# Chunk one's keys and queries by seven block products, key roundings shared between two engines, early stores in halves, and a new order of the work

## The chip, the cores and the metric

The kernel runs on one core of a Trainium2 chip. A core has five engines that run side by side, each through its own queue in order: TensorE (PE, matrix products into PSUM; its weight loads are listed apart as PEld), VectorE (DVE), ScalarE (ACT), GpSimd (POOL), and SyncE (SP), which here only issues DMAs. Semaphores order work across engines. The metric is the device time of one execution in microseconds (us), the median of several runs.

## The reference, cut to what matters

Inputs are x (2048 rows of 512), one fused weight for queries, keys and values, a small 16 x 16 weight for each of 32 heads, an output weight, the two weights of a dense layer of 1376 units, and a gate vector.

```python
qkv = (x @ wqkv) ...                                  # 32 heads of 16
pq, pk = q @ w_phi, k @ w_phi                         # per head
phi(p) = concat(softmax(p), softmax(-p))              # 32 features per head
kv, z = phi_k^T v, sum over rows of phi_k
a = (phi_q kv) / (phi_q z + 1e-6) @ wo                # linear attention
b = mish(x @ w1 + b1) @ w2                            # dense, Mish, dense
out = g * a + (1 - g) * b,  g = sigmoid(x . gate_w)
```

Everything is float32.

## The kernel before, in words

**Precision.** A float32 matrix is split into a high part (rounded to the matmul's format) and a low part (the rest). A product of two such matrices is three matmul passes: high x high, high x low, low x high. In the steps' names an h is a rounding to the high part and an l the subtraction that leaves the low part.

**Stages.** P0 prepares weights. It multiplies the key and query weights by each head's w_phi on PE (steps fk0 to fk3 and fq0 to fq3, lines 943 to 950; one for each of four row blocks of the weight, loaded by lk and lq), so that x times the fused weight gives pk or pq at once. The fused weights lie in PSUM; kh, qh round them into SBUF (line 966), kl, ql subtract (line 967), kr, qr copy them unrounded (line 970). A step's last two digits are the part (rows 0, 1, or 2 and 3 of the four) and the half r of the columns. In step, chunk 0's keys are computed as the weights come: `p0a0` is part 0, pass a (high x high; b is high x low, c is low x high), row tile 0.

Stage A goes through eight chunks of 256 rows (two tiles of 128). For each: keys k, queries q and values v (12 matmuls each per tile: three passes by four row blocks), the key features (mx, mn, d, E, S, rS, ml: maximum, minimum, differences, exp, sum, reciprocal, scaling), kv and z sums; queries are parked in DRAM (qe copies, st stores).

Stage B goes through four blocks of 512 rows: up (x @ w1, 11 units), Mish on ACT (mi), splitting (h, l), down (dn, w2), query features, numerators (nu), output product (wo), gate (gr, gs, ge, gg), the mix (ag on ACT, fi on DVE) and the stores (so, lines 890 to 892). Stage B's first units begin before stage A ends.

**Seven products.** For a chunk in FAST (line 35) keys and queries come by a scheme of seven block products (fast_ops, from line 386): with two row tiles, two halves of the 512 inner rows, and key and query weights side by side, the eight block products of the plain way become seven, s1 to s7, of 6 matmuls each. They need sums of blocks of x (sa: four additions; sh, sl: their split) and sums of blocks of the weights: t1 to t4 (lines 351 to 361), built from the unrounded copies kr and qr and split by W:h0 to h3 and W:l0 to l3. bc and m7 copy partial results on ACT; ca and qa combine them on DVE. Before, chunks 2 to 7 are in FAST; chunks 0 and 1 go the plain way.

**What sets the order.** ORDER (line 41) is a list of steps written out by hand or by a program; each engine takes its steps in the order of the list (pin, line 104). `@` gives the buffer slots that a step's new tiles take, a trailing v or g says whether VectorE or GpSimd does it, and `^` makes a GpSimd step wait until the VectorE step listed before it has ended. A tile in a reused slot waits until all readers of the slot's earlier tile are done. The loads of weights, of x and of stored results all go through SP's queue in the order of the list.

The WARM matmuls (line 192) on a tile of ones run while the first loads come.

Of the kernel before, what the change touches and what calls it, by code (L numbers as in the profile page):

```python
# [39 lines left out]
SLOTS = "01201010215"  # L40
ORDER = """
    P0| w0 lk0 lk1 fk0@01 kh00 fk1 lx0@0 xh0 kh01 kl01 kl00 p0a0@0 kr00 p0a1@1 kr01 xl0g^ lk2 fk2@23 lk3 kh10 kl10 fk3 lx1 xh1 lx2 p0b1 p0c1 kh11 kl11 p0b0 p1a1 kh20
    P0| p0c0 p1b1 xl1v p1c1 p1a0 kh21 p1b0 kl21 xh2 p1c0 p2a0 kl20 p2a1 p2b1 ldx@1 A0:xh@3467 xl2v p2c1 A0:xl0g^ kr11 A0:mn1@0 A0:d11@0 A0:mx1@0 A0:d01 kr10 lv0@0 p2b0
    P0| p2c0 A0:mx0@1 A0:d00@1 lq2 vh0 fq2@01 lq3 fq3 qr11 lq0 fq0@32 lq1 fq1 qh01 qr01 A0:xl1g A1:k0@2 A1:k1@1 qh10 qh11 ql11 A0:mn0@1 qh00 ql00 A0:ldx@0 A0:d10 lv1@1
    P0| vh1 vl0g qr10 A1:sag@1 A1:sh0 W:L1@0 vl1v A0:v1@1 A0:E0 qr00 W:t1v ql01 ql10 A0:q0@0 A0:qe0@0 W:t4v W:t3g^ A0:E1 A0:st0 A1:sh1 A1:sl0v A1:mx0@0 A1:mn0@0 A0:v0
    A1| d10@2 d00 E0 A0:ve1@3 A0:S1@0 W:h0 A0:q1@0 sl1g mx1@1 W:h1 W:t2 xh@0215 v0@3 ve0@1 A0:S0@1 A0:rS0 A0:qe1@1 A0:st1 A0:ml0v xl0v mn1@1 d11@3 xl1v W:h2 W:l2g W:l1v
    A1| q1@2 S0@1 qe1@0 A0:z0 v1@2 A2:s1@01 A2:bc@0 q0@2 ldx@1 A2:sag@0 W:H1 qe0@1 rS0 A0:ve0@2 A2:xh@3467 ml0v st0 A0:rS1 A0:ml1v A0:z1 st1 A2:xl0v A2:s6 W:h3 W:l0v
    A2| W:l3g A1:d01 s7 m7@1 ca@2 xl1g A1:E1 A1:S1@1 s2 mn0@0 v0@3 ve0@0 A3:s1@11 A1:rS1 s5 qa W:L7@1 W:H7 s4 sh0 sl0g^ A3:s7 A3:m7@0 A1:z0 A3:bc@3 s3 A1:ml1g^ A1:z1
    A2| mx0@0 sh1 W:O1g st1 mx1@1 d11@1 d10@0 A1:ve1@2 kk mn1@1 d01 E1 A3:s6 d00 E0 A3:ca@2 W:O7g^ A3:v0@1 A3:ve0@3 ldx@1 A3:xh@0251 A3:xl1g A3:sag^@0 A3:sh0 W:L2@0 W:H2
    A3| A2:v1@2 A2:ve1@1 A2:S0@0 xl0g A2:sl1v s5 s2 A2:rS0 A2:ml0v A2:z0 A2:S1@1 A2:rS1 qa st1 s4 s3 sh1 qe0@1 mn0@0 d10@2 mx1@1 d11@3 W:L0@1 sl0v mx0@0 d00 A4:s1@01  # L50
    A4| s7 bc@2 s6 A3:sl1g m7@0 A3:mn1@1 A3:d01 A3:E1 ca@1 s2 mx0@1 mn0@0 s5 qa A3:ldx@1 A2:ml1g^ A3:v1@3 A2:z1 A3:E0 st1 A3:st0 sag^@0 s4 W:H0 A3:S0@0 A3:rS0 A3:ml0g^
    A4| xh@3467 s3 sh1 A3:S1@1 A3:rS1 A3:ml1v xl0v A3:z1 sl1g xl1v A3:ve1@2 d10@0 qe0@0 d00 kk E0 v0@1 ve0@0 mn1@1 d01@1 A5:s1@22 sh0 mx1@0 v1@3 W:O0v A2:qe0@1 A2:st0
    A4| A3:z0 sl0g d11 E1 S1@0 rS1 ml1g^ z1 S0@1 A5:s7 A5:bc@1 A5:s2 A5:mn0@0 ldx@1 A5:xh@0251 A5:xl0g W:L6@1 rS0 ml0v A5:s6 A5:v1@0 A5:m7@1 A5:ca@0 W:H6 z0 A5:s5
    A5| sag^@0 s4 A4:st0 W:O2v qa s3 sh1 st1 mx0@1 d00@3 d10 xl1v A4:ve1@1 sl1g sh0 sl0v mn1@1 mx1@0 d11@2 v0@2 W:L4@0 ldx@1 qe0@0 st0 A6:s1@13 E0 S0@0 A6:sag^@0 A6:s7
    A6| bc@1 s6 m7@1 ca@2 xh@3476 A5:d01 A5:rS0 xl1g s2 A5:zld s5 qa st1 A5:E1 A5:S1@1 mn0@0 B0:LX0@1 xl0g^ A5:rS1 s4 A5:ml0v A5:ml1v sh0 sl0g s3 qe0@0 A7:s1@03 sh1
    A6| W:O6v A7:s7 A5:za A5:z0g A7:bc@1 mx0@1 st0 A7:s2 mx1@0 d11@0 A5:ve0@3 sl1v mn1@1 A5:ve1@2 kk d01 A5:z1g^ W:L8@1 A7:m7@1 A7:s6 A7:ca@2 B0:XH0 B0:XL0v v0@2 ve0@0
    A7| mx0@0 B0:LX1@0 B0:XH1 B0:XL1g^ A6:d10@1 s5 qa st1 s4 W:H4 W:H8 d00@3 W:O8g mx1@0 s3 d11@2 mn0@1 A6:v1@0 A6:d00 A6:E0 qe0@0 st0 mn1@0 d01 A6:E1 A6:S0@0 A6:rS0 E1
    A7| A6:ve1@1 W:O4g B0:lq0@1 A6:S1@1 A6:rS1 A6:ml1v B0:up1@1 B0:mi1@0 A6:ml0v W:L3@1 B0:h1@2 B0:l1v@5 A6:z0g S1@1 B0:lq2@0 B0:mx2@0 d10 v0@3 ve0@3 rS1 A6:z1v ml1g E0
    B0| A7:S0@0 A7:rS0 A7:ml0v A7:z0v up3@2 mi3@1 up0@1 mi0@0 mn2@0 A7:v1@2 A7:ve1@2 up5@0 W:L5@0 h3@3 l3v@4 ha@7 A7:z1v dn1b@1 hb@6 W:wm ph A7:zh1@10 d02v@1 A6:kv A7:kv
    B0| W:H5 dn3c@0 up2@2 dn3b mn0@1 W:H3 A7:zl1v mx0@1 pi dn0c A7:zh0 A7:zl0v A7:z0b@3 W:O5v dn1d@2 mi2@1 dn0b d00v@0 d12v A7:zc0 d10g W:O3v E0 pc A7:z1b@3 A7:zc1 T0v@1  # L60
    B0| lq1@1 mx1@0 up4@2 mn1@1 gr@0 W:L9@0 D0@0 d11g@3 dn3d dn1a@3 E2 mi4@0 dn1c h4@2 dn0ad dn3a T2v@0 up8@1 l4v@5 h2@7 l2g^@6 dn2bcd dn4d dn2a W:L10@1 W:H10 dn4c mi8@3
    B0| W:H9 h8@4 S0@1 m0 W:O9g de0 rd0 up6@2 sc0 es0v tr0 S2@0 up7@1 d01v dn4a gs up9@0 mi5@0 h5@1 l5g@7 dn5bad W:O10v E1 T1g@1 ge mi6@6 lq3@0 mn3@0 dn4b l8g^@0 dn8b
    B0| h6@3 mx3@1 d03g@2 dn5c l6g^@2 dn6ab A7:ldo@0 A7:WH1 dn6c mi7@5 h7@1 S1@1 D1@1 m1 de1 up10@2 dn6d l7g@6 dn7a W:L11@1 W:H11 B1:lq0@1 B1:mn0@1 d13g mi9@7 h9@5 st0
    B0| ld0 rd1 dn7c sc1 es1v tr1 st1 l9g^@3 dn7b dn9da D2@0 dn7d m2 de2 dn9c B1:LX0@1 rd2 W:O11v dn8c E3 dn8d A6:ldw1@1 sc2 A7:km@0 A7:kt es2v tr2 st2 dn9b mi10@2 h10@7
    B0| l10g@1 dn10a dn8a B1:lq1@0 S3@1 T3v@0 D3@1 m3 de3 rd3 sc3 es3v tr3 WL1v A7:WH0 dc A7:kc ld1 nu0@1 oh0@01 WL0v ol0 dn10bd gg0 B1:XH0 B1:XL0v dn10c ld2 wo1@0 ag1@1
    B1| B0:fi1 LX1@0 B0:wo0 d10v@0 XH1 mx1@0 d01g@3 XL1v up0@2 B0:st3 B0:ld3 B0:so1 B0:nu1@1 B0:ag0@3 B0:fi0 mn1@0 d11g B0:oh1@01 B0:ol1 E1 S1@0 up1@0 lq3@0 up2@1 mi2@6
    B1| B0:wo2 h2@2 l2g^@5 dn2ca@13 mx0@1 up6@1 d00v E0 T0g^@1 B0:ag2@2 mi1@3 dn2d@0 B0:fi2 S0@1 h1@4 l1g@0 B0:wo3@0 dn1d D0@0 dn1c mi0@7 up5@0 up3@1 hb@1 ha@6 B2:lq1@1
    B1| dn2b@2 B2:mn1@1 B2:d11v@1 ph pi pc B0:so0 dn0c T1g@0 dn0b dn1a B0:ag3@0 dn1b B0:fi3 mn3@0 B2:mx1@0 mi6@3 h6@7 B2:d01g m0 D1@1 de0 up7@0 mx3@1 l6v@2 dn6c rd0 dn6a
    B1| mi5@5 lq2@1 mn2@1 d13g@2 mx2@0 h5@3 l5g^@4 dn0a dn5b dn0d dn5d m1 de1 rd1 sc1 es1g tr1 st1 mi3@0 h3@5 dn5c l3g^@6 dn3d gr@0 dn6d B0:so2 sc0 dn3c gs dn3a up8@1
    B1| mi7@1 dn5a es0g d03v E3 S3@0 up4@2 mi8@0 h8@3 dn3b B3:lq1@0 l8v@4 dn8c d12g@3 up9@0 B2:LX0@1 tr0 d02v dn8d h7@0 l7g^@5 dn7ab T3v@0 D3@1 dn6b dn7c st0 m3 de3 rd3  # L70
    B1| up10@1 ge B3:mn1@0 sc3 E2 T2v@0 D2@0 es3g ld0 mi4@6 h4@1 l4v@7 mi10@2 h10@6 l10g@0 B2:XH0 mi9@5 S2@1 dn4d dn8a dn7d dn8b ld1 nu0@2 oh0@01 m2 dc dn4c dn10ab de2
    B1| rd2 dn10d h9@3 l9g@4 dn9adc sc2 es2v tr3 B2:LX1@0 B2:XH1 B2:XL1g dn4a B2:XL0v B2:up0@1 ol0 B2:mi0@2 wo1@0 B2:ha@5 B2:lq3@1 B2:mx3@1 dn9b B2:d03g@0 B2:mn3@1
    B2| up1@2 B1:tr2 E1 d13v E3 B1:gg0 B1:st2 B1:dn10c mi1@3 lq0@1 mx0@0 mn0@1 d10g@3 T1v@1 B1:ag1@1 B1:wo0 B1:ag0@3 up3@2 mi3@4 pc B1:st3 B1:ld2 B1:ld3 B1:nu1@0 B1:dn4b
    B2| B1:oh1@01 B1:fi1 B1:fi0 up5@2 B1:so0 B1:ol1 h1@6 l1g^@0 dn1d@2 S1@0 hb@1 B3:d11g@2 dn1c@3 h3@7 l3v@3 B1:wo3@0 mi5@4 B1:wo2 B1:ag3@2 B1:fi3 dn1b@0 T3g^@0 up4@2 pi
    B2| ph dn0cb D1@1 d00g^ m1 de1 E0 rd1 T0g@1 up2@0 sc1 es1g dn0a@1 B1:ag2@3 B1:fi2 gr@1 D3@0 gs mi4@2 B1:so2 S3@1 m3 dn0d de3 up8@1 ge dn1a rd3 sc3 h5@5 l5v@1 dn5a
    B2| up6@2 mi6@4 dn3b tr1 dn5b S0@0 dn5d h6@6 D0@1 m0 de0 rd0 sc0 dn3c es0g^ dn5c dn3da B3:LX0@0 up10@2 h4@0 l4g^@5 dn4b mi2@1 h2@7 es3v dn4c l2g^@2 dn4d lq2@1 mx2@1
    B2| mn2@1 d12g^@1 dn2bad st1 up7@0 ld1 l6g@3 dn6ad d02g dn6b dn2c tr0 B3:mx1@0 st0 B3:d01v dn4a mi8@1 h8@4 l8v@7 E2 dn8d up9@1 dn8a B3:lq3@0 T2g@1 ld0 nu0@2 D2@0
    B2| mi10@2 dn6c S2@1 m2 de2 mi7@0 h7@1 l7v@5 dn7a dn8c B0:so3 dn7d mi9@0 h9@6 l9g^@3 dn9db B3:LX1@1 dn9a tr3 rd2 sc2 es2v B3:mx3@0 h10@0 tr2 st2 ld2 dn9c B3:XH0
    B3| B2:oh0@01 B2:dn7c B2:l10v@6 B2:dn10cad XH1 B2:ol0 XL1v XL0v up1@0 E1 up0@1 mi0@3 S1@0 mn3@0 d13g@3 T1g@1 mi1@2 B2:wo0 d03v h1@0 l1g^@6 B2:gg0 B2:ag0@3 B2:dn10b
    B3| lq2@1 mn2@1 B1:so3 mx2@1 hb@2 d12v@1 d02v E2 S2@1 T2g^@0 B2:wo1@2 B2:ag1@0 B2:dn8b up3@0 gr@0 B2:dn7b B2:dc D2@1 B2:fi1 B1:so1 mi3@4 B2:st3 B2:ld3 m2 B2:nu1@2  # L80
    B3| B2:oh1@01 B2:ol1 up7@1 lq0@1 mx0@0 up4@0 gs dn1d@0 B2:wo3@2 mi4@7 B2:wo2 de2 D1@0 m1 rd2 de1 d00v@0 h4@1 mn0@0 d10v l4v@5 B2:fi0 dn4b@1 dn1b rd1 sc1 es1v up5@0
    B3| dn4d ha@7 pi ph dn0dabc@32 sc2 up10@2 B2:ag2@2 B2:fi2 B2:ag3@1 B2:fi3 tr1 B2:so0 dn1a E3 T3v@0 mi5@2 dn4c h5@3 l5g^@7 dn5b dn4a up6@0 h3@2 st1 l3g@1 dn3db dn5d
# [951 lines left out]
```

## Time and profile before

| | us |
|---|---|
| median of three runs | 442.8 (442.55 to 443.0) |
| profiled execution, its own time | 442.08 |
| its span in the profile | 440.4 |
| PE busy | 434.0 |
| DVE, ACT, POOL busy | 315.7, 232.7, 186.2 |

The span is the time from the first to the last instruction that the profiler saw; the execution's own time is a little longer. Matmuls are pipelined: one takes some 0.39 us from start to end, but the next starts earlier, so the piece of the chain that holds a run of them, divided by their number, is what one costs. "Chain" is the chain of work that ended last, followed back from the last instruction to what released it.

### The profile page before, as it was taken

What the parts mean: (1) busy time and instruction counts of PE and PEld (TensorE: products, weight loads), DVE (VectorE), ACT (ScalarE), POOL (GpSimd) and SP (SyncE); (2) the same over time, 40 slices, a digit from 0 to 9 for tenths busy, and PEclk for the clock granted to TensorE, in tenths of its full rate; (3) what the DMA queues carried; (4) which work ended last, traced back from release to release, by engine and by line L of the source; (5) the groups of instructions that cost most, each with busy time, mean ns of one, the idle gap of its engine ahead of it and who ended that gap; (6) DMA issues with size and microseconds to landing.
All of it is one profiled execution on the core that took longest, in us unless ns stands there. A gap on an engine that the chain in (4) does not pass through costs nothing.

```text
span 440.4 us, 7237 instructions
## 1 busy us (share of the span) xinstructions
PE 434.0 (99%) x2841; PEld 353.1 (80%) x2841; DVE 315.7 (72%) x435; ACT 232.7 (53%) x317; POOL 186.2 (42%) x143
## 2 busy tenths in 40 slices
...
GB/s 265 239 25 119 146 172 144 164 222 207 173 165 168 37 121 25 190 236 220 48 50 24 106 149 104 216 25 2 190 146 48 192 96 2 71 119 100 164 1 119
DMA packets 29321, 55.14 MB, mean 125 GB/s; under 512 B 5284, under 2 KB 13988, under 8 KB 29288
## 3 DMA queue, kind: packets, MB, share of 16 engines
...
## 4 chain that ended last, share of the span: by engine, by line
PE 98%; ACT 1%; DVE 0%; issue 0%; DVEq 0%
PE proj L129 28%; PE up L129 27%; PE down L129 27%; PE wo L129 10%; PE num L129 2%; PE kvp L129 2%; PE warm L129 1%; PE fuse L129 1%; ACT wkh L156 0%; ACT w1bhf L156 0%; PE z L129 0%; DVE wkl L967 0%; ACT io L156 0%; DVE io L888 0%; PE kvT L656 0%
## 5 line engine op out<-in xcount | busy, mean ns | idle before, releaser
L707 POOL TENSOR_TENSOR l<-act,h 128x512 fp32r<-128x512 f32 x25 | 34.0, 1362 | 107.7 <-ACT h L156 44.0
L156 ACT ACTIVATE act<-up,cst 128x512 f32<-128x512 f32 x44 | 29.9, 687 | 59.9 <-PE up L129 39.4
L319 DVE TENSOR_REDUCE Sm<-E 128x64 f32<-128x1024 f32 x32 | 38.5, 1202 | 17.6 <-ACT E L156 17.6
L156 ACT ACT_TABLE_LOAD x35 | 44.9, 1283 | 4.2 <-PE up L129 2.9
L156 ACT ACTIVATE E<-E 128x1024 f32<-128x1024 f32 x32 | 33.5, 1058 | 16.1 <-DVE E L313 5.8
L129 PE MATMUL wo<-woh,ohl 128*128 128x512 f32 x128 | 41.5, 389 | 0.0
L156 ACT ACTIVATE h<-act 128x512 fp32r<-128x512 f32 (+1 forms) x48 | 29.6, 630 | 21.1 <-POOL l L707 7.8
L129 PE MATMUL down<-w2ah,h 128*128 128x512 f32 x96 | 37.8, 394 | 0.0
L129 PE MATMUL down<-w2al,h 128*128 128x512 f32 x96 | 37.4, 389 | 0.0
L129 PE MATMUL down<-w2bh,h 128*128 128x512 f32 (+1 forms) x81 | 31.8, 392 | 0.0
L129 PE MATMUL down<-w2bh,l 128*128 128x512 f32 (+1 forms) x81 | 31.3, 387 | 0.0
L129 PE MATMUL down<-w2bl,h 128*128 128x512 f32 (+1 forms) x81 | 31.3, 387 | 0.0
L129 PE MATMUL down<-w2ah,l 128*128 128x512 f32 x80 | 31.2, 391 | 0.0
L888 DVE SCALAR_TENSOR_TENSOR io<-down,cst,io 128x512 f32<-128x512 f32 (+1 forms) x17 | 11.8, 715 | 26.3 <-ACT io L156 12.6
L707 DVE TENSOR_TENSOR l<-act,h 128x512 fp32r<-128x512 f32 x15 | 10.8, 720 | 24.3 <-PE down L129 15.9
L129 PEld LDWEIGHTS wo<-woh,ohl 128*128 128x128 f32 x128 | 24.0, 188 | 5.0
L794 POOL TENSOR_TENSOR T<-E,zb 128x1024 f32<-128x1024 f32 x9 | 22.0, 2446 | 11.0 <-ACT E L156 8.0
L129 PE MATMUL up<-xbh,w1ahr 128*128 128x512 f32 x96 | 25.8, 391 | 0.0
L129 PE MATMUL up<-xbh,w1alr 128*128 128x512 f32 x96 | 25.7, 389 | 0.0
L129 PE MATMUL up<-xbl,w1ahr 128*128 128x512 f32 x96 | 25.7, 389 | 0.0
L129 PE MATMUL wo<-wol,ohl 128*128 128x512 f32 x64 | 24.9, 389 | 0.0
L156 ACT ACTIVATE io<-wo,cst 128x512 f32<-128x512 f32 x16 | 10.8, 684 | 24.9 <-PE wo L129 24.9
...
## 6 DMA issues: line engine op xcount, KB each, us to landing
...
eT<-eTd SPq DMA_DIRECT2D x64, 128.0 KB, 2.7
...
pqd<-qs SPq DMA_DIRECT2D x16, 256.0 KB, 3.3
pq<-pqd SPq DMA_DIRECT2D x16, 256.0 KB, 3.5
out_dram<-io SPq DMA_DIRECT2D x15, 256.0 KB, 2.4
...
```

Of the source, the lines that this page charges most:

```text
L129: return pin(nc.tensor.matmul(*a, **k))
L156: return pin(A_.activation(out_, in_, fn, **k))
L319: pin(V.tensor_reduce(d["S"], hv(d["E"][:, :]), axis=AX.X, op=ALU.add))
L707: on_(e)(e.tensor_sub(U[i]["l"], U[i]["a"], f32(U[i]["h"])))
L794: on_(e)(e.tensor_mul(d["T"], d["E"], B["zb"]))
L888: pin(V.scalar_tensor_tensor(io[t][:, sl], dn[t][:, sl], og_sb[:, i % 8 : i % 8 + 1], io[t][:, sl], op0=ALU.mult, op1=ALU.add))
```

## The change

- FAST becomes chunks 1 to 7: chunk 1's keys and queries, too, go by s1 to s7. Its plain steps k0, k1, q0, q1 and the copy qe1 go; s1 to s7, bc, m7, ca, qa come, and in chunk 0's steps the operands sa, sh0, sh1, sl0, sl1 for it. The sums of the operands are done by VectorE (sav), as are W's four low parts (two before).
- The roundings kh01 and kh11 (column half 1 of the first two row blocks of the key weight) are done by VectorE (a copy from PSUM) in place of ScalarE.
- The stores of output tiles 0 to 4 (block 0's four and block 1's first) are issued as two DMAs of 256 columns each.
- The step w0, which issued no matmul, is gone; the nine warm matmuls stay.
- ORDER is new as a whole: the order of the loads in P0, of the steps in all stages, and the choice between VectorE and GpSimd and of slots for many steps; SLOTS differs in its last digit.

```diff
-WARM = 9, 0
-FAST = range(2, 8)
+WARM = 9
+FAST = range(1, 8)
-SLOTS = "01201010215"
+SLOTS = "01201010213"
 ORDER = """
-    P0| w0 lk0 lk1 fk0@01 kh00 fk1 lx0@0 xh0 kh01 kl01 kl00 p0a0@0 kr00 p0a1@1 kr01 xl0g^ lk2 fk2@23 lk3 kh10 kl10 fk3 lx1 xh1 lx2 p0b1 p0c1 kh11 kl11 p0b0 p1a1 kh20
...
+    P0| lk0 fk0@01 lx0@0 xh0 xl0g kh01 kl01 lk2 fk2@23 kh00 p0a0@0 kl00 p0a1@1 p0b1 lx1 xh1 lk1 xl1g^ fk1 kh11 kh10 lk3 fk3 kl10 lx2 xh2 kh21 lq3 kl11 p0c1 kl21 p1a1
+    P0| kh20 kl20 xl2g^ kr01 ldx@1 A0:sav@0 A0:xh@4576 A0:xl1v A0:xl0v p0b0 p0c0 p1a0 p1b0 kr11 lv1@0 vh1 kr00 p1c0 p1b1 p1c1 p2a1 p2b1 p2c1 A0:mx1@0 kr10 p2a0 p2b0 p2c0
+    P0| A0:mx0@1 lv0@1 vh0 A1:s1@20 A0:mn1@0 lq2 fq2@13 lq0 fq3 qr11 fq0@02 qr10 lq1 fq1 qh01 qr01 vl1g vl0v W:L7@0 A0:v0 A0:mn0@1 qh11 A0:d00@0 ql01 qr00 qh00 ql00
+    W| t1v h0 t3v A0:d01@1 P0:qh10 P0:ql10 A0:d10 A1:v1@2 L1@1 t4g P0:ql11 t2 h3 l0v l3v A1:v0@0 A1:ve0@3 h1 h2 l2v l1v A0:ldx@1 A0:q1@0 A0:qe1@0 A0:st1 A0:sh1 A0:sl1v
+    A1| A0:v1@1 A0:E0 A0:S0@0 A0:ve1@1 bc@3 A0:q0@0 s2 xh@4702 xl0g A0:sh0 A0:sl0g s7 m7@1 mn0@1 d10@2 A0:qe0@0 s6 A2:s1@00 A2:bc@1 xl1g mx0@1 d00 ca@2 A0:d11 sag@0 sh0
...
-    def warm(j):
-        for _ in range(WARM[j]):
-            mm(wps[:, :P], ones, ones, start=True, stop=True)
-
-    warm(0)
+    for _ in range(WARM):
+        mm(wps[:, :P], ones, ones, start=True, stop=True)
...
-                for sl in cols(t):
+                for sl in cols(t) if i > 4 else (slice(0, 256), slice(256, 512)):
                     pin(Sy.dma_start(out[i * P : (i + 1) * P, sl], io[t][:, sl]))
...
-    at(PRE, "w0", lambda: warm(1))
...
-                at(PRE, f"{n}h{j}{r}", lambda h=h, ps=ps: act(h, ps()))
+                if n == "k" and j < 2 and r:
+                    at(PRE, f"{n}h{j}{r}", lambda h=h, ps=ps: pin(V.tensor_copy(h, ps())))
+                else:
+                    at(PRE, f"{n}h{j}{r}", lambda h=h, ps=ps: act(h, ps()))
```

More of the change, by code (lines that the diff above doesn't have):

```diff
@@ L32 @@
 GROW = REST = FA % P
-WARM = 9, 0
-FAST = range(2, 8)
+WARM = 9
+FAST = range(1, 8)
 SUM = 5
-SLOTS = "01201010215"
+SLOTS = "01201010213"
 ORDER = """
-    P0| w0 lk0 lk1 fk0@01 kh00 fk1 lx0@0 xh0 kh01 kl01 kl00 p0a0@0 kr00 p0a1@1 kr01 xl0g^ lk2 fk2@23 lk3 kh10 kl10 fk3 lx1 xh1 lx2 p0b1 p0c1 kh11 kl11 p0b0 p1a1 kh20
[L43 to L82, printed above, removed]
-    B3| dn3c dn1c up9@2 dn5a E0 T0g@1 mi10@5 es2v tr2 pc dn3a st2 ld1 up2@2 S0@0 D0@0 m0 h10@4 l10v@0 dn10a de0 rd0 mi9@6 h9@5 l9g^@2 dn9d ge dn9abc dn10db sc0 es0v tr0
-    B3| S3@1 gg0 mi2@1 h2@6 l2g^@5 dn2c D3@1 m3 dn10c dn2bd de3 rd3 B2:so1 sc3 mi7@2 es3v st0 ld0 nu0@2 dn2a up8@1 B2:so3 mi6@1 h6@4 oh0@01 tr3 st3 ld3 ol0 wo1@0 mi8@0
-    B3| h8@6 l8v@5 dn5c dn8c h7@0 wo0 l7v@3 ag0@3 l6g^@7 dn6b dc ld2 nu1@2 oh1@01 dn6a ag1@0 dn6c dn7db dn8a dn7a ol1 wo2 ag2@1 dn7c fi0 so0 dn8b B2:so2 fi1 so1 fi2
-    B3| wo3@1 dn8d so2 ag3@3 dn6d fi3 so3
@@ new lines @@
+    W| t1v h0 t3v A0:d01@1 P0:qh10 P0:ql10 A0:d10 A1:v1@2 L1@1 t4g P0:ql11 t2 h3 l0v l3v A1:v0@0 A1:ve0@3 h1 h2 l2v l1v A0:ldx@1 A0:q1@0 A0:qe1@0 A0:st1 A0:sh1 A0:sl1v
+    A1| A0:v1@1 A0:E0 A0:S0@0 A0:ve1@1 bc@3 A0:q0@0 s2 xh@4702 xl0g A0:sh0 A0:sl0g s7 m7@1 mn0@1 d10@2 A0:qe0@0 s6 A2:s1@00 A2:bc@1 xl1g mx0@1 d00 ca@2 A0:d11 sag@0 sh0
+    A1| sl0g A0:rS0 A0:ml0g^ A0:z0 s5 A0:E1 E0 qa S0@1 s4 mn1@1 s3 sh1 sl1g ldx@1 A2:xh@1356 A0:S1@0 A0:rS1 A2:s2 A2:mn0@0 A0:ml1v A2:s7 d01@3 A0:z1 A2:m7@0 A2:s6
@@ new lines @@
+    A2| ca@1 A0:ve0@2 v0@0 ve0@0 xl0g^ s5 xl1g^ mx0@0 A0:st0 A1:mx1@1 sag@0 qa A1:d11 A1:E1 A1:S1@0 A1:rS0 A1:rS1 sh0 sl0g^ A1:ml0v A1:ml1v s4 mn1@1 d01@0 v1@0 mx1@1 d11
+    A3| A2:s3 A2:qe0@1 A2:sh1 s1@22 bc@1 A1:ve1@2 A2:kk A1:z0 A1:st1 s2 A2:ve1@1 s7 mn0@1 m7@0 A2:ldx@1 xh@4702 A2:sl1v mx0@1 d00@1 A2:d10@2 s6 ca@1 A2:st1 A1:z1 v0@0
+    A3| A2:st0 sag@0 s5 xl0g s4 A2:E1 A2:S1@1 A4:s1@22 A2:rS1 A2:ml1g ve0@3 d10 A2:z1 W:H1 sh0 E0 sl0g A2:d00 A2:E0 W:O1g^ qa st1 s3 A4:s7 v1@0 A4:m7@1 A4:bc@2 xl1v
@@ new lines @@
+    A4| A1:qe0@0 A3:sh1 A3:sl1g A3:mn1@0 A2:S0@0 A2:rS0 A3:ldx@1 A3:S0@1 W:L0@1 A2:ml0v A3:d01@3 A3:rS0 A2:z0 A3:ml0v s2 xh@1365 xl1g^ mn0@1 xl0g s6 v0@3 ca@0 s5
+    A4| A5:s1@12 ve0@2 A1:st0 W:H7 sag^@0 sh0 mx0@1 A3:mx1@0 A3:d11 qa s3 st1 A3:E1 A3:S1@0 s4 mn1@0 ldx@1 A3:z0 sl0g A3:rS1 A3:ml1v A5:bc@3 A5:s2 qe0@0 sh1 W:H0 W:O0v
+    A4| A3:ve1@0 kk A5:s6 d00@2 d10 st0 E0 mx1@0 d11@0 A5:s7 W:O7g^ A5:m7@1 sl1g A5:ca@2 v1@0 A5:s5 A3:z1 d01 A5:s4 A5:sag@0 A5:sh0 A5:sl0g^ E1 A5:mn0@1 A5:d10@1 A5:v0@2
@@ new lines @@
+    A5| xh@4702 xl0g mx0@1 d00 E0 W:L2@1 qa s3 W:H2 st1 W:L6@0 ve0@1 qe0@0 A4:S0@1 A4:rS0 S0@0 xl1g^ A6:s1@03 A4:ml0v A4:z0 A4:S1@1 rS0 sh1 mx1@0 sl1g A4:ve1@3 mn1@0
+    A6| A5:d01@3 W:O2g^ A4:rS1 A4:ml1v A4:z1 v0@2 W:H6 W:O6v A3:qe0@1 A3:st0 ve0@0 A5:d11 s7 bc@0 m7@1 s2 s6 ca@1 A5:ldx@1 sav@0 A5:E1 A5:S1@1 A5:v1@1 mn0@1 xh@1356
+    A6| xl1g^ xl0g^ sh0 s4 W:L8@1 A5:rS1 A5:ml1g^ A5:zld s5 A5:za B0:LX0@1 W:L5@0 sl0v mx0@1 A7:s1@22 A7:s7 qa st1 mn1@0 W:H8 W:O8v W:wm A5:ml0v A5:z0g A5:z1g A5:st0
@@ new lines @@
+    A7| bc@3 s2 A5:ve1@2 mx0@0 d00@2 A6:d10@0 mn0@1 d10 A6:s3 A6:qe0@1 A6:sh1 A6:sl1v A6:kk m7@0 s6 ca@2 A6:st0 A6:mx1@0 B0:LX1@0 E0 A6:d00 A6:E0 A6:v1@1 S0@1 rS0 B0:XH0
+    A7| B0:XL0g B0:XH1 B0:XL1g^ B0:lq2@1 s5 A6:d01@1 W:L4@1 s4 mx1@1 W:H4 v0@0 v1@2 A6:d11 A6:E1 W:H5 A6:S0@0 qa s3 A6:rS0 mn1@1 d01@3 B0:mn2@0 st1 d11 E1 B0:up0@0
+    B0| gr@0 gs mi0@4 hb@7 ha@0 A7:qe0@0 A6:ml0v A7:st0 A7:ml0v A7:S1@0 A7:rS1 up5@1 W:O5v W:O4v up3@2 mx2@0 mi5@2 up4@0 A6:ve1@3 A6:S1@1 A6:rS1 A6:ml1v up1@1 ge mi3@1
```

28 lines of the change are left out of this document (added).

## Prediction

> **What bounds the kernel now.** I read the page first (busy time, then the chain that ended last), then who TensorE waited for, the chain in order of time, and the busy time by stage.
>
> ```profile
> PE 434.0 (99%) x2841; PEld 353.1 (80%) x2841; DVE 315.7 (72%) x435; ACT 232.7 (53%) x317; POOL 186.2 (42%) x143
> ...
> PE 98%; ACT 1%; DVE 0%; issue 0%; DVEq 0%
> ```
>
> 98% of the chain is TensorE (PE), so what a matmul costs in the chain is what it costs in time. The chain in order of time shows where it is not PE, and what the pieces cost:
>
> ```profile
> 1.12 4.21 PE warm L129 x18
> 5.34 1.07 PE fuse L129 x30
> 6.43 0.39 ACT wkh L156
> 6.87 0.77 PE fuse L129 x32
> 8.07 0.77 DVE wkl L967 x2
> 8.86 1.08 ACT w1bhf L156 x2
> 9.95 1.05 ACT wkh L156 x3
> 11.03 4.57 PE proj L129 x19
> 15.60 2.02 PE fuse L129 x128
> 17.63 42.39 PE proj L129 x186
> 146.92 2.72 PE proj L129 x12
> ```
>
> From 11.03 us the chain stays on PE until the last products. Before that it leaves PE for ScalarE (ACT) and VectorE (DVE): the fused key weights are computed, rounded and split there, and the keys of chunk 0 wait. The busy time by stage (the columns are the stretch, its length, then PE, weight loads, DVE, ACT, GpSimd (POOL), clock, DMA) says the same:
>
> ```profile
> 5.27:11.03 5.76, 4.54 (x134) 3.33 (x134) 1.82 (x6) 2.94 (x8) 0.73 (x1) 1.00 1.00 359
> 11.03:17.56 6.53, 6.53 (x148) 5.42 (x148) 5.13 (x10) 4.52 (x8) 4.02 (x3) 1.00 0.85 315
> 17.56:436.34 418.78, 418.78 (x2549) 340.43 (x2543) 307.71 (x418) 223.64 (x300) 178.71 (x128) 1.00 0.39 119
> ```
>
> After 17.56 PE is busy for 418.78 of 418.78 us at the full granted clock (1.00). So two things can move the time: fewer matmuls, and an earlier start of the dense stretch. Everything else can only spoil it.
>
> **The change, part by part.** *Seven block products for chunk 1.* Its keys and queries now take 4 x 12 = 48 matmuls, seven products of 6 take 42. Twelve proj matmuls take 2.72 us (last row above), 0.227 each, so 6 fewer save 1.36 us.
>
> The Trainium skill (Perfetto Trace Analysis, section Identifying the Most-Contended Engine) warns that matmul busy time is a bad measure of headroom and that the weight loads' busy share is the good one. Here that share is 80%, and if it were the limit the removed matmuls would give nothing; that result is rival 3.
>
> What the products add elsewhere: two more copies on ACT (bc, m7) and two operand roundings less one query copy, a combination on DVE (ca, qa), four sums and two differences for the operands.
>
> ```profile
> L156 ACT ACTIVATE proj<-proj 128x512 f32<-128x512 f32 x6 | 3.5, 584 | 5.5 <-PE proj L129 5.5
> L156 ACT ACTIVATE w2bh<-sraw 128x512 fp32r<-128x512 f32 x6 | 3.8, 630 | 3.5 <-POOL sraw L378 3.5
> L422 DVE TENSOR_TENSOR proj<-proj,qs 128x512 f32<-128x512 f32 x6 | 4.2, 694 | 2.5 <-PE proj L129 2.3
> ...
> 36.00:60.00 24.00, 24.00 (x110) 19.59 (x113) 19.10 (x23) 12.95 (x21) 15.93 (x13) 1.00 0.45 146
> ```
>
> ACT gets about 3 x 0.6 = 1.8 us more in a stretch where it is busy 12.95 of 24; DVE gets 2 x 0.69 where it idles 4.9. Both are covered there. Over the whole order, steps counted by engine and priced by such rows, DVE gets some 1 us more, ACT 1, POOL 4, in 440: nothing, unless a single step comes late. If cover is gone, each us by which a step comes late is a us of PE.
>
> *The head.* The new order loads wk piece 0, x piece 0, wk piece 2, x piece 1, wk 1, wk 3, x piece 2. Landings now, by issue and median time to landing:
>
> ```profile
> 0.81 0.87 SPq L236 DMA_DIRECT2D w1ahf<-in_wkT_dram  x2
> 1.72 0.43 SPq L232 DMA_DIRECT2D xraw<-in_xT_dram  x1
> 2.19 0.91 SPq L236 DMA_DIRECT2D w1ahf<-in_wkT_dram  x2
> 3.14 0.92 SPq L232 DMA_DIRECT2D xraw<-in_xT_dram  x2
> ...
> 6.09 2.58 SPq L236 DMA_DIRECT2D w1alf<-in_wqT_dram  x4
> ...
> xraw<-in_xT_dram SPq DMA_DIRECT2D x1, 128.0 KB, 4.8
> ...
> w1ahf<-in_wkT_dram SPq DMA_DIRECT2D x2, 256.0 KB, 5.7
> ...
> xraw<-in_xT_dram SPq DMA_DIRECT2D x1, 256.0 KB, 6.0
> ...
> w1alf<-in_wqT_dram SPq DMA_DIRECT2D x1, 256.0 KB, 7.8
> ```
>
> SyncE issues one about every 0.46 us, and the fourth row's second issue is at 3.62. So 640 KB of the queue (wk 0, wk 1, x 0) are in at 1.72 + 4.8 = 6.5; 1152 KB (through wk 3, issued 2.67) at 8.3; 1536 KB (through x 2) at 9.6; 3584 KB (the last of four wq pieces, issued 8.3, 0.3 before that row ends) at 16.1. I read the new landings off this line: wk 2 (640 KB) 6.5, wk 1 (1024) 7.9, wk 3 (1280) 8.8, x 2 (1536) 9.6. Durations for what follows:
>
> ```profile
> 6.43 0.38 ACT L156 ACTIVATE wkh<-fuse 128x256 fp32r<-128x256 f32 x1 [3.59 <-PE fuse L129]
> 6.56 0.29 DVE L932 CAST xh<-xraw 128x256 fp32r<-128x256 f32 x1 [5.49 <-DMA xraw<-in_xT_dram]
> 10.26 0.42 DVE L967 TENSOR_TENSOR wkl<-fuse,wkh 128x256 fp32r<-128x256 f32 x1 [1.43 <-ACT wkh L156]
> 11.13 0.41 DVE L936 TENSOR_TENSOR xl<-xraw,xh 128x256 fp32r<-128x256 f32 x1
> 11.32 1.71 ACT L156 ACTIVATE xh<-xraw 128x512 fp32r<-128x512 f32 x3
> 11.52 1.29 DVE L967 TENSOR_TENSOR wkl<-fuse,wkh 128x512 fp32r<-128x512 f32 x2
> 13.84 1.11 ACT L156 ACTIVATE wvh<-raw 128x1024 fp32r<-128x1024 f32 x1
> ```
>
> A rounding of fused keys on DVE is in no row: 0.29 (the cast from SBUF) is the lower bound, 0.42 (a DVE instruction that reads the fused PSUM) the upper; I take 0.42, because the source is the same PSUM.
>
> Step by step: fk0 still ends at 6.41, behind the same warm matmuls. ACT rounds one half to 6.8 while DVE rounds the other to 6.85; DVE's two wkl end at 7.65. PE does fk2 meanwhile (6.6 to 7.35), then three chunk-0 products to 8.1. fk1 needs wk 1 (7.9) and those wkl: 8.2 to 8.75. fk3 needs wk 3 (8.8): to 9.4. Now the rest, 21 key products, can run from 9.45, with about 0.1 lost at the turn: 9.45 + 21 x 0.227 + 0.1 = 14.3. What must keep up: x 2 rounded on ACT from 9.65, the two last roundings (about 0.57 each by the x3 row) to 11.25, DVE's two wkl to 12.05. The products that need the former begin at 11.6, the latter at 12.05. Covered, by 0.35 and by nothing; if ACT slips 0.3, PE slips with it.
>
> So the key products, which end with the 4.57 piece at 15.60 now, would end at 14.3. Then chunk 1's first product (6 matmuls, 1.36) runs to 15.7, before the query fusions. Its operands' sums (four on DVE, 4 x 0.4 from 12.05) end at 13.6, its two xl at 14.3 and 14.95; it needs the low one at 15.25.
>
> The query fusions are next: the queue's 3584 KB now end with lq2 (2816 did before), which thus lands at 16.1, and the last, lq1 (4096 KB, at the same slope of 0.8 us per 256 KB), at 17.7. PE asks for them at 16.0 and 17.5. So they end near 18.2 rather than 17.63, with 1.36 us of matmuls more behind them: a head gain of 17.63 + 1.36 - 18.2 = 0.8 us. Bounds: 1.1 if loads come a little earlier, since then DVE's 12.05 holds; -0.5 if loads are 1.3 us later, which goes straight into PE.
>
> *The block operands' tops (t1 to t4) come some 10 us earlier.* After 18.2 PE has v0 of chunk 0, v1 and v0 of chunk 1 (8.16 us) before the queries of chunk 0 at 26.4. Those need DVE's last reading of chunk 0's keys and their second query split. Counting DVE's steps from 14.95 by 0.68 per 512-wide and 1.22 per 1024-wide step, with 0.45 lost waiting for ACT, they are done at 26.1 and 26.7; the latter is asked for at 27.3. Slack 0.3 and 0.6. The first seven-product matmuls that need a top come at 35.9, DVE's last low part at 32.8. Covered, narrowly at 26.
>
> *The remaining edits.* The halved stores are five more issues of about 0.4 us on SyncE, which no chain piece names; stores wait for landing behind PE by tens of us there: nothing (five times 0.4 = 2 us at most, if every one held up a load). w0 issues no matmul. The tail keeps its shape: halved last unit, fi, so. Nothing.
>
> Sum, against the profiled execution's own 442.08 us (span 440.4 and 1.7 around it): -1.36 - 0.8 = -2.2, thus 439.9. That execution ran 0.7 below the median of the three timed runs, 442.8; on that scale I forecast **440.6 us**.
>
> **Rivals** (times on the median's scale). *1, the port that VectorE and GpSimd share, ending slower.* Two rows of now show it:
>
> ```profile
> 39.05 2.40 POOL L361 TENSOR_TENSOR w1blr<-w1blf,w2bl 128x1024 fp32r<-128x1024 f32 x1 [5.88 <-ACT w2bl L156]
> 39.71 2.28 DVE L297 TENSOR_TENSOR xl<-xraw,xh 128x512 fp32r<-128x512 f32 x1
> ...
> 37.79 0.69 DVE L297 TENSOR_TENSOR xl<-xraw,xh 128x512 fp32r<-128x512 f32 x1
> ...
> 16.04 2.37 POOL L941 TENSOR_TENSOR wvl<-raw,wvh 128x1024 fp32r<-128x1024 f32 x1
> ```
>
> A DVE step on two SBUF operands takes 0.69 alone and 2.28 when a POOL step is under way: it waits until that ends. In the new order wvl (2.37 on POOL) meets chunk 1's second xl at 14.3: it is ready when ACT's wvh ends, 1.11 us after wv 1 lands (2816 KB: 13.7 by the line above, earlier if the loads run as evenly as before 9.6). If POOL is first, xl ends at 17.4 instead of 14.95 and the block product stands from 15.25 on: 2.1 us. The same again at 22.5, where t4's sum on POOL meets t3 on DVE: DVE is 2.4 late, the slack of 0.3 to 0.6 takes some, 1.9 us. Both: +4.0 - 2.2 = +1.8, thus 444.6. It decides when POOL gets the port first at both; against it, by that line wvh ends at 14.8, after DVE's second xl has begun, and at 22.5 DVE's t3 stands ready at once while POOL still waits for t1's end to be signalled. One of the two alone gives about -0.1, 442.7: no change. The Trainium skill (GPSIMD Engine Reference, section 1. Specifications) states such a sharing for two SBUF inputs; by the rows above the trace agrees.
>
> *2, the head gains nothing.* Loads or ACT late by 0.8 in the head: -1.36 alone, 441.4. For it: the landings carry every step up to 17.7. Against: the line they are read from.
>
> *3, PE has slack.* Then the 1.36 is not had and only the head's 0.8 stays: 442.0. Against it stand the matmuls 0.227 apart with no idle time over 418.78 us.
>
> *4, the block products don't do what they say*, because PE waits for their operands (ca before s4, slack some 1.2 us by the same count): a stall of 1.4 eats the saving, 442.0.
>
> **Chances.** Forecast 0.48 (439.6 to 441.0); rival 2 0.20; one port clash, rivals 3 and 4 together 0.19, all near no change; rival 1 in full, or several us of late loads, 0.10; below 439.6 0.03. A measurement of this kernel tells 0.2%, 0.9 us, from no change: faster is below 441.9, slower above 443.7. Range 439.3 to 443.0, which leaves out rival 1 and little else; the forecast's own is 439.6 to 441.0.
>
> **What would show it.** Right: proj rows of chunk 0's keys ending near 14.3; the query fusions ending near 18.2; no PE wait after that; 6 proj matmuls fewer. Wrong: an idle PE before the fusions (loads) or before the first block product or the chunk-0 queries (the port: look for DVE xl or w1bhf rows of over 2 us), or new PE waits in chunks 1 to 3 on ca, sraw or xl. The prediction fails if the new order makes PE wait anywhere after 18 us for more than 1 us, which no row of now can show.

## The result and the profile after

The changed kernel takes 439.58 us (median; 439.27 to 439.81) against 442.77 for the kernel before (442.55 to 443.0): ratio 0.9927, 95% interval 0.991 to 0.9945, so 3.2 us faster. Forecast was 440.6, with a range of 439.3 to 443.0. Ratios, here and below, are drawn from all executions of both kernels in one session but for a few that ran far longer, so they can differ a little from the quotient of the two medians. The profiled execution took 439.43 us (before: 442.08), its span is 437.7 (before: 440.4). The spans differ by 2.7; the other 0.5 of the 3.2 is the place of the two profiled executions among their kernels' others: that of before lay 0.7 under its median, that of after 0.15.

The page of the changed kernel, busy time and shares of the chain that ended last:

```profile
PE 432.8 (99%) x2835; PEld 352.0 (80%) x2835; DVE 319.9 (73%) x441; ACT 231.4 (53%) x317; POOL 182.3 (42%) x147
...
PE 99%; DVE 0%; DVEq 0%; issue 0%
```

Six matmuls fewer, and no other engine is left in the chain. Who TensorE waited for, whole span (total, times, longest, us):

```profile
PE warm L130 <- DVE ones L190: 1.1, 1, 1.1
```

That is the wait for the first operand at the very start. The three waits of the kernel before for ScalarE's wkh (0.8 and 0.5 us in all) are gone and no new one came. The chain in order of time (start, us, what):

```profile
5.38 1.60 PE fuse L130 x64
...
7.05 1.19 PE proj L130 x3
8.25 1.09 PE fuse L130 x64
9.34 6.36 PE proj L130 x27
15.70 2.02 PE fuse L130 x128
17.73 41.14 PE proj L130 x180
```

The 27 are chunk 0's last 21 key matmuls and the six of chunk 1's first block product. By stage (stretch, its length, then PE, weight loads, DVE, ACT, POOL, clock, DMA share, GB/s):

```profile
9.34:15.63 6.29, 6.29 (x27) 4.92 (x28) 5.78 (x13) 5.61 (x11) 2.20 (x2) 1.00 0.86 338
...
17.66:434.01 416.35, 416.35 (x2536) 338.16 (x2531) 309.24 (x419) 221.65 (x301) 174.42 (x131) 1.00 0.40 120
```

The end of the query fusions divides the span. **Up to it**, 17.66 now against 17.56 then: 0.1 later, with 1.36 us of matmuls more done, a gain of 1.26. (Counted from each kernel's first fusion, which began 0.11 later now, it is 1.37; in the runs below that leave the head as it is, 1.23 to 1.59.) **From it to the last matmul**, 416.35 against 418.78: 2.43 less. Twelve matmuls left this stretch, six that are gone and six that went ahead of the fusions, 2.72 at 0.227; so 0.29 came in. From one matmul's start to the next, 0.22 of it stands where one kind of matmul follows another: such steps lie 1.67 us in all above 0.227 each, 1.45 before. Why they grew is not shown. **After the last matmul**, 440.37 - 436.34 = 4.03 then, 437.69 - 434.01 = 3.68 now: 0.35 less. Together: -1.36 (removed) - 1.26 (head) + 0.29 - 0.35 = -2.68. The last two terms were forecast as nothing.

### The profile page after: what moved, and what is told of

It is laid out like the page before. It is cut to its first block, busy times and chain, and to the rows that moved or that the text cites. A ratio compares the mean times of both kernels' runs of the same rounds, so it can differ in the third digit from the quotient of the medians.

```text
span 437.7 us, 7246 instructions
## 1 busy us (share of the span) xinstructions
PE 432.8 (99%) x2835; PEld 352.0 (80%) x2835; DVE 319.9 (73%) x441; ACT 231.4 (53%) x317; POOL 182.3 (42%) x147
## 4 chain that ended last, share of the span: by engine, by line
PE 99%; DVE 0%; DVEq 0%; issue 0%
PE proj L130 28%; PE up L130 28%; PE down L130 27%; PE wo L130 10%; PE num L130 2%; PE kvp L130 2%; PE fuse L130 1%; PE warm L130 1%; PE z L130 0%; DVE io L886 0%; PE kvT L654 0%; DVEq L1030 0%; DVE ones L190 0%
## 5 line engine op out<-in xcount | busy, mean ns | idle before, releaser
L705 POOL TENSOR_TENSOR l<-act,h 128x512 fp32r<-128x512 f32 x28 | 37.7, 1346 | 117.9 <-ACT h L157 37.5
L836 DVE STREAM_TRANSPOSE E<-E 128x1024 f32<-128x1024 f32 x16 | 19.9, 1243 | 10.3 <-POOL E L333 10.0
L130 PEld LDWEIGHTS down<-w2ah,h 128*128 128x128 f32 x96 | 18.0, 188 | 5.6 <-issue 1.2
L796 DVE TENSOR_REDUCE Dn<-T 128x64 f32<-128x1024 f32 x16 | 19.3, 1208 | 4.3 <-POOL T L792 4.0
```

What stands on the lines that cost most here:

```text
L130: return pin(nc.tensor.matmul(*a, **k))
L705: on_(e)(e.tensor_sub(U[i]["l"], U[i]["a"], f32(U[i]["h"])))
L796: pin(V.tensor_reduce(d["D"], hv(d["T"][:, :]), axis=AX.X, op=ALU.add))
L836: at(key, f"tr{t}", lambda d=d: pin(V.transpose(d["E"][:, :], d["E"][:, :])))
```

## The experiments

Beside the times stand the chain and the waits of each profiled execution; TensorE's first fusion starts anywhere from 5.27 to 5.75 us, with the landing of the first loads, so lengths between two places of the chain are compared, rather than spans: from the last query-fusion matmul to the last matmul of all, start to start (in words: from the fusions to the last matmul), and from the last matmul's start to the end of the span (the end).

**The changed kernel again**, as a base:

> The changed kernel itself, to have its interval against the kernel before and its trace beside the others. Two terms are known from the traces: 6 matmuls fewer (1.36 us) and the fusions of the query weights ending at the same 17.7 us with 1.36 us of chunk 1's product already done (1.3 us of head). If these two are all, the gain is 2.4 to 2.8 us. If a third source exists outside PE's sequence (the end, or the launch), the gain is 3.0 to 3.4 us and the span's end after the last matmul is shorter by the difference in every run.

439.38 us (439.25 to 439.75), ratio 0.9912 (0.9888 to 0.9937). From the fusions to the last matmul it takes 416.26 us, in the first profile 416.22; the end takes 3.96 in both. So lengths read this way repeat to 0.04.

**What a matmul is worth: one product twice.**

```diff
         def s7():
-            term("m7", lambda: s(0), t3, True, True)
+            for _ in range(2 if c == 1 else 1):
+                term("m7", lambda: s(0), t3, True, True)
```

> The changed kernel with one of chunk 1's seven products done twice over the same PSUM, the second overwriting the first: six matmuls more, no other step added and none moved. Theory (a matmul costs its 0.227 us wherever PE has no idle time): the last matmul starts 1.36 us later, 417.6 us after the query fusions end against 416.22; span 439.05 to 439.4; time about 440.8. Rival (the engine has slack, since its weight loads are busy only 80% of the span): 416.2 to 416.5, time about 439.5.

440.85 us (440.82 to 441.51); span 439.1. By stage, TensorE alone, from the fusions' end to the end of the last matmul:

```profile
17.70:435.44 417.74, 417.74 (x2543) 1.00 0.40 120
```

417.74 against 416.35: 1.39 for six matmuls, and still no wait. The six cost what the prediction took off (1.36), so TensorE has no slack there, whatever the share of the weight loads (80% in both).

**The change without the seven products of chunk 1.** The new order with FAST from chunk 2, chunk 1's steps k0, k1, q0, q1 in place of its products:

```diff
-FAST = range(1, 8)
+FAST = range(2, 8)
-    ... A0:xl1v A0:xl0v ... A1:s1@20 ... A1| ... bc@3 A0:q0@0 s2 xh@4702 ... s7 m7@1 ...
+    ... A0:xl1v A0:xl0v ... A1:k0@2 ... A1| ... A0:q0@0 xh@4702 ... k1@2 sag@0 q0@1 ... q1@1
```

> The changed kernel with chunk 1's keys and queries by 48 plain matmuls again (its operand sums and splits are gone, its steps are put in between chunk 0's queries and chunk 2's first products). Theory (PE's own work sets the time): 1.36 us slower than the changed kernel plus whatever PE waits the trace shows, which an order not fitted to it may have. Rival (the removed matmuls' time was hidden, and the gain is all from the order of the head): the same as the changed kernel within 0.4 us.

446.67 us (445.04 to 446.98), 7 more than the changed kernel. Four of the six executions took 446.4 to 447.0 at a mean granted clock of 0.994 to 0.996; the profiled one took 445.21 at 0.998, 5.8 more than the profiled one of the changed kernel. Its chain in the head (start, us, what):

```profile
9.40 7.74 PE proj L130 x33
```

The waits, besides that of the start:

```profile
PE proj L130 <- ACT qs L157: 2.3, 1, 2.3
PE proj L130 <- DVE E L311: 1.6, 1, 1.6
```

33 matmuls take 7.74 where 27 took 6.36: again 1.38 for six. The rest are stalls of an order that wasn't fitted to this form: a key product whose PSUM DVE had not yet finished reading (E, 1.6), and a copy of queries on ScalarE behind the rounding of an input that SyncE had asked for only after the store of other queries (qs, 2.3). So this run doesn't price the products by its time alone.

**The same, with two moves against the stalls.**

```diff
-    ... xl1g k1@2 sag@0 q0@1 sh0 qe0@0 ... mn1@1 sh1 sl1g ldx@1 A2:xh@1356
+    ... xl1g q0@1 sag@0 k1@2 sh0 ldx@1 qe0@0 ... mn1@1 sh1 sl1g A2:xh@1356
```

> As the run with chunk 1 by plain products (span 443.5, last matmul started 420.58 us after the query fusions ended, against 416.22 in the changed kernel), with two moves that should end its two stalls: the next input of chunk 1's turn is asked for before the store of its queries, and one query product goes ahead of the key product that waited 1.6 us. Theory (a removed matmul is worth its 0.227 us on the path): six more matmuls, so last matmul 417.6 us after the fusions end, span 439.1 to 439.4, time about 440.8. Rival (the seven products are worth nothing because the engine is held by something else): span 438.0, as the changed kernel. Rival (the plain form stalls in any order): over 441.

443.47 us (443.16 to 444.85), ratio 1.0019 (1.0002 to 1.0037): the expected 440.8 was missed, and the rival that the plain form stalls here too (over 441) came. The earlier load ended the 2.3 us stall; the other move only passed the wait on to the query product, which needs PSUM that DVE frees later still:

```profile
PE proj L130 <- DVE E L313: 2.2, 1, 2.2
```

And this stall cost more than its length. TensorE by stage around it (stretch, length, PE busy, clock, DMA share, GB/s):

```profile
33.00:35.80 2.80, 2.80 (x13) 1.00 0.00 0
35.80:38.03 2.23, 0.05 (x2) 0.98 0.29 109
38.03:40.00 1.97, 1.97 (x5) 0.50 0.03 9
40.00:42.00 2.00, 2.00 (x8) 0.66 0.07 16
42.00:44.00 2.00, 2.00 (x11) 1.00 0.67 246
```

After 2.2 us without matmuls the granted clock is 0.50 and then 0.66: 0.50 x 1.97 + 0.34 x 2.00 = 1.7 us lost on top. From the fusions to the last matmul this execution takes 420.10, 3.88 more than the changed kernel with as many matmuls there; stall (2.2) and slow clock (1.7) make 3.9. Four of the twelve executions, this one among them, took 444.6 to 444.9 at a mean granted clock of 0.994 to 0.996, and eight 443.2 to 443.5 at 0.998 to 1.000, so the loss does not come with every execution. What the pair shows: with plain products in this order the waits, not the six matmuls, make the difference, and the six are 1.36 to 1.39 wherever they can be read alone.

**The new head in the old order.** P0's first loads, roundings and key products as in the change, the two key roundings on VectorE, all else as before:

```diff
-    P0| w0 lk0 lk1 fk0@01 kh00 fk1 lx0@0 ... lk2 fk2@23 lk3 kh10 kl10 fk3 lx1 xh1 lx2 ...
+    P0| lk0 fk0@01 lx0@0 ... lk2 fk2@23 ... lx1 xh1 lk1 xl1g fk1 kh11 kh10 lk3 fk3 kl10 lx2 xh2 kh21 lq3 ...
```

> The kernel before with only the new head: the new order of loads and of chunk 0's key steps, and the two roundings on VectorE; chunk 1 plain, stages A and B in the old order. Theory: the query fusions end near 16.3 instead of 17.6 us and the whole is 1.3 us faster than before. Rival (the head's gain is taken back, since the old order's VectorE and ScalarE steps behind it do not come earlier with it): new PE waits in the first 60 us, and a gain under 0.4 us.

442.18 us, 0.5 under the 442.71 of the kernel before in the same session; ratio 0.9975 (0.9957 to 0.9992), which is 1.1 us; span 439.8 against 440.4. Of the expected 1.3 us less came, and of the rival (under 0.4) more. Its chain around the fusions:

```profile
6.82 7.87 DMA w1alf<-in_wqT_dram
14.69 0.14 issue
14.82 2.10 PE fuse L129 x128
16.92 42.39 PE proj L129 x186
```

The timeline's row of its fusions, with the idle time before them and what ended it:

```profile
14.82 2.10 PE L129 MATMUL fuse<-bds,w1alf 64*64 64x64 f32 x128 [0.64 <-DMA w1alf<-in_wqT_dram]
```

and that of the kernel before, with no idle time:

```profile
15.53 2.10 PE L129 MATMUL fuse<-bds,w1alf 64*64 64x64 f32 x128
```

The keys end 1.35 us earlier (14.82 - 0.64 = 14.18, against 15.53), as forecast; then the query pieces are not there and 0.6 of it is lost, so the fusions end 0.71 earlier (16.92 against 17.63). Counted from each one's first fusion (5.51 here, 5.27 before) the head alone gives 0.95, where with the product ahead of the fusions it gives 1.37. In the changed kernel the first block product fills the time of that wait; the two parts of the change need each other.

**The old order of loads in the new kernel.**

```diff
-    P0| lk0 fk0@01 lx0@0 xh0 xl0g kh01 kl01 lk2 ... lx1 xh1 lk1 xl1g^ fk1 kh11 kh10 lk3 fk3
+    P0| lk0 fk0@01 lk1 lx0@0 xh0 xl0g kh01 kl01 lk2 lk3 ... lx1 xh1 xl1g^ fk1 kh11 kh10 fk3
```

> The changed kernel with the first seven loads in the old sequence (wk 0, wk 1, x 0, wk 2, wk 3, x 1, x 2). Theory (the head's gain comes from the loads' sequence: fk2 runs while the first fused part is rounded): fk2 waits until some 7.2 us instead of 6.1, the dense stretch of PE starts 0.3 to 0.5 us later, and the whole is that much slower than the changed kernel. Rival (the sequence of PE's steps alone makes the gain, whatever the loads): the same within 0.15 us.

440.4 us (439.83 to 442.13), ratio 0.9943 (0.9921 to 0.9965). Three of the eight executions took 441.6 to 442.1 at a mean granted clock of 0.994 to 0.996; the median of the other five is 439.93. In the profile, which is one of the five:

```profile
PE fuse L130 <- DMA w1ahf<-in_wkT_dram: 1.1, 1, 1.1
```

TensorE waits 1.1 us for wk piece 2, which this order loads after piece 1; the 27 matmuls start at 9.88 against 9.34 and the fusions end 0.54 later (18.27 against 17.73). So of the 1.26 about half hangs on the order of the loads.

**Both key roundings back on ScalarE** (`if n == "k" and j < 2 and r` never taken):

> The changed kernel with the two key roundings kh01 and kh11 back on ScalarE, all else as it is. Theory (the step is off the path, since the next load lands later than the rounding ends): ScalarE does two roundings of 0.38 us in a row instead of one, the low parts and fk1 come at most 0.1 us later, the time is the same within 0.2 us. Rival (the roundings are on the path of the head): both delays add up and the time is 0.4 to 0.8 us longer.

439.65 us (439.51 to 440.13), ratio 0.9941 (0.9927 to 0.9954): no difference from the changed kernel, and the keys and the block product end at 15.69 (15.70 there). In this execution the query pieces then landed 0.55 later than in the changed kernel, and the fusions waited 0.33 for one; that is not the roundings' doing, but it shows how near this load is. The roundings on VectorE in the changed kernel take 0.42, the upper of the two bounds of the prediction (`x2`: least, median, most in ns):

```profile
L964 DVE CAST wkh<-fuse x2: 423/424/424, 6.5 to 9.0; 128x256 fp32r<-128x256 f32 x2
```

Which of the two engines does them is not worth anything here.

**One port clash made on purpose.** VectorE's d01 moved between the sums t1 and t3, so that GpSimd's t4 comes first:

```diff
-    W| t1v h0 t3v A0:d01@1 P0:qh10
+    W| t1v A0:d01@1 h0 t3v P0:qh10
```

> The changed kernel with one VectorE step moved: chunk 0's d01 (0.68 us, reads PSUM) between t1 and t3. So GpSimd's second sum for t4 starts before VectorE's t3. Theory (a GpSimd step and a VectorE step on two SBUF operands exclude each other for a whole step): t3, 1.23 us now, shows some 3.2 us; the last difference of chunk 0's first tile ends near 27.3 instead of 25.3, chunk 0's queries start 1.4 us late, and the whole is 1.2 to 1.6 us slower than the changed kernel. Rival (they share without excluding): t3 under 1.6 us, no PE wait, the same time within 0.2 us.

440.99 us (440.64 to 441.56), ratio 0.9966 (0.9953 to 0.9979). GpSimd's and VectorE's sums, here:

```profile
22.45 2.40 POOL L351 TENSOR_TENSOR w1bhf<-w1bhf 128x1024 f32<-128x1024 f32 x1 [1.97 <-DVE w1bhf L353]
22.82 3.11 DVE L354 TENSOR_TENSOR w1blf<-w1blf 128x1024 f32<-128x1024 f32 x1
```

and in the changed kernel:

```profile
22.29 1.23 DVE L354 TENSOR_TENSOR w1blf<-w1blf 128x1024 f32<-128x1024 f32 x1
22.40 3.39 POOL L351 TENSOR_TENSOR w1bhf<-w1bhf 128x1024 f32<-128x1024 f32 x1 [1.93 <-DVE w1bhf L353]
```

Whoever starts first runs at its own speed, and the other waits until about its end (0.13 to 0.15 us less than in full): 0.11 us ahead, VectorE takes 1.23 and GpSimd 3.39; 0.37 us behind, VectorE takes 3.11 and GpSimd 2.40. TensorE then stood before chunk 0's queries, where the prediction put it:

```profile
PE proj L130 <- DVE E L313: 1.1, 1, 1.1
```

From the fusions to the last matmul it takes 1.46 us more (417.68 against 416.22); t3 took 1.88 longer, of which a slack of 0.64 (below) takes its part. Rival 1 was a real risk, with its mechanism and place right, and the order of the change escapes it by 0.11 us.

**The first five stores whole again** (`for sl in cols(t)`):

> The changed kernel with the first five output tiles stored whole: five DMA issues of some 0.4 us fewer on SyncE. Theory (stores lie off the path): the same within 0.2 us. Rival (the halves decide which later DMAs wait for which, since DMAs take turns on a few completion semaphores): PE waits in stage B appear, 0.3 us or more slower.

440.07 us (439.77 to 440.8), ratio 0.9951 (0.9936 to 0.9965): 0.5 to 0.7 more than the changed kernel, where at most 0.2 was expected, and without the waits in stage B of the rival. Its head and its dense stretch are those of the changed kernel to 0.02 us, yet the end takes 4.29 us where that of the changed kernel takes 3.96. So does every kernel with whole stores so far (before 4.31, the new head in the old order 4.31), and every one with halves takes 3.95 or 3.96. The tiles in question are stored some 50 us before the end and earlier. SyncE's closing waits from the last landing on (line, queue, kind, count: ns least/median/most, first and last start), first in this kernel:

```profile
L1030 SPq EVENT_SEMAPHORE  x6: 28/28/28, 436.9 to 437.2; - x6
```

and in the changed one:

```profile
L1030 SPq EVENT_SEMAPHORE  x1: 28/28/28, 436.8 to 436.8; - x1
```

At the end SyncE goes through a list of waits, one instruction some 0.06 us after the other. When the last store lands, the whole-store kernel stands at a wait with five more behind it, 5 x 0.06 = 0.3; the changed kernel stands at the last of the list.

Two runs test that. **The kernel before with the five halves and nothing else:**

```diff
-                for sl in cols(t):
+                for sl in cols(t) if i > 4 else (slice(0, 256), slice(256, 512)):
```

> The kernel before with nothing but its first five output tiles stored in halves. In the traces so far the end (last matmul's start to the end of the span) is 4.29 to 4.31 us in all three kernels with whole stores and 3.95 to 3.96 in all six with halves, though the halved tiles are stored long before. Theory: SyncE's last waits are one instruction each about 0.06 us apart, one after the other over the semaphores that stores use in turn; five more stores move the last store from the fifth wait to the tenth and last, so nothing is left to step through after it lands: end 3.96, span about 440.0 against 440.4, time -0.3. Rival (the shorter end comes from the new order of work, not from the halves): end 4.31, time unchanged.

442.24 us, ratio 0.9987 (0.9977 to 0.9997). One wait is left after the last landing, and the end takes 3.97:

```profile
L1030 SPq EVENT_SEMAPHORE  x1: 28/28/28, 440.0 to 440.0; - x1
```

(The forecast of the end, 3.96, holds; that of the span, 440.0, doesn't. It is 440.9: the first fusion began 0.34 later than in the kernel before, with the landing of its load, and the stretch from the fusions to the last matmul is 0.50 longer, 0.33 of it a wait for a copy of queries.) **The changed kernel with six halves** (`i > 5`):

> The changed kernel with six output tiles stored in halves instead of five. Theory of the wait list: one store more moves the last store on by one place, from the tenth wait round to the third; after it lands seven waits of about 0.06 us are still to be stepped through: end 4.35 to 4.4 us against 3.96, span about 438.2 to 438.4. Rival (halved stores shorten the end by being smaller or earlier): end 3.96 or a little less, span 437.7 to 438.0.

440.09 us (439.78 to 441.39), ratio 0.9945 (0.9926 to 0.9964); the end takes 4.38, forecast 4.35 to 4.4, with eight waits from the last landing on:

```profile
L1030 SPq EVENT_SEMAPHORE  x8: 28/28/28, 436.9 to 437.3; - x8
```

Counts of 6, 1 and 8 with none, five and six more stores fit eight places used in turn. So the number of transfers on the queue counts, though the halved ones land long before the end; that it counts modulo eight rests on these three numbers. No run beat the changed kernel.

## Why the prediction was right, and where not

**Bound by TensorE: right.** No wait after the start; the doubled product cost 1.39 us. Rival 3 (slack in TensorE) falls. The Trainium skill (Perfetto Trace Analysis, section Identifying the Most-Contended Engine) would have headroom on TensorE read from the weight loads' busy share, here 80%, and from the share of peak arithmetic. The run with six more matmuls shows no headroom behind the 80%.

**Seven products, -1.36: right**, and rival 4 (products stalled on their operands) falls: no proj row waits. That the products add nothing elsewhere holds but for the 0.29 us of the dense stretch, which was not in the sum and whose cause stays open.

**The head, 0.8: right in mechanism, too small; 1.26 was measured.** Key matmuls before the fusions: the keys and the block product end at 15.63, forecast 15.7. The term that was mis-sized is the landing of the query pieces, forecast at 16.1 (lq2) and 17.7 (lq1). The rows of the changed kernel:

```profile
7.18 1.62 SPq L234 DMA_DIRECT2D w1alf<-in_wqT_dram  x3
...
DMA to landing us min/median/max: 8.1/8.1/8.2
```

The three issues, at 7.18, 7.82 and 8.47, landed 8.1 to 8.2 us later, at 15.3, 16.0 and 16.6: 0.65 us per 256 KB, where the line through the landings of before gave 0.8. The trace of before had that number: its own four query pieces land from 14.15 to 16.11, 0.65 apart, but the line was drawn over the longer stretch from 9.6. And the first 3584 KB, which end with lq2, were in 0.8 sooner than in the kernel before; why is not shown. So the fusions start at once and end at 17.66 rather than 18.2. The bound of 1.1 for "loads a little earlier" does not follow from the forecast's own steps either: keys to 14.3, the product to 15.7 and 2.02 of fusions end at 17.7 if no load is waited for, which is a gain of 1.3. Rival 2 (the head gains nothing) falls, though the head alone, without the block product, does lose 0.6 of its 1.35 to exactly these loads.

**The tops, slack 0.3 and 0.6 at 26: covered, as forecast, with more to spare.** DVE's d10 and chunk 0's queries in the changed kernel:

```profile
24.63 0.68 DVE L313 TENSOR_TENSOR E<-mn,proj 128x512 f32<-128x512 f32 x1
...
25.95 1.07 PE L130 MATMUL proj<-wqh,xh 128*128 128x512 f32 x4
```

d10 ends at 25.31, 0.64 ahead of the queries; the second query split ends at 25.90, 0.96 ahead of the first matmuls on the low parts of the query weight. The clash run used the first up: 1.9 late, 1.46 lost.

**Rival 1, two port clashes: neither came as told.** At 14.3 both VectorE's xl were done before GpSimd's wvl began:

```profile
13.31 1.29 DVE L295 TENSOR_TENSOR xl<-xraw,xh 128x512 fp32r<-128x512 f32 x2
...
14.74 2.39 POOL L939 TENSOR_TENSOR wvl<-raw,wvh 128x1024 fp32r<-128x1024 f32 x1 [3.54 <-ACT wvh L157]
```

13.31 + 1.29 = 14.60: a margin of 0.14. At 22.3 VectorE was first, as the prediction argued, by 0.11; GpSimd took the wait (3.39 where it takes 2.40), and TensorE waited for nothing.

**The halved stores, "nothing": wrong.** They are 0.35 of the 2.68. The step that failed is the sum's reason for putting them at nothing, that stores wait for their landing behind TensorE by tens of us. The halved stores are indeed early: in the changed kernel the last of them is issued at 383 us, and stores land 1.7 to 4.2 us after their issue. But the gain isn't there; it is in the list of waits after the last landing, which the trace of before showed (six of them, 0.06 apart) and the prediction did not read.

**The number: inside the range, but not where it was put.** 439.58 lies just under the forecast's own band, 439.6 to 441.0; times below 439.6 had been given a chance of 0.03. On the profile's own scale the forecast was -2.2 and -2.7 came: 0.46 more in the head, 0.35 at the end, 0.29 lost in the dense stretch. On the scale of the medians 0.5 more came, because the profiled execution of before lay further under its median than that of after. So the range held with a term in it that was not foreseen.
